# An xLSTM block, a top-2 expert layer and an ELU feed-forward on one core: summed logits in PSUM, a repeated block of 64 columns, more work allowed on GpSimd, and a new order

## The chip, the cores and the metric

The kernel runs on one core of one Trainium2 chip. The metric is the device time of one execution in microseconds (us); less is better. The time before is the median of three runs.

## The reference, cut to what matters

Three layers follow each other on 1536 tokens of 320 values: a gated linear attention (2 batches, 8 heads, 768 steps, 40 wide), a router that sends each token to two of eight experts (320 x 1024 x 320), and a dense layer (320 x 2048 x 320) with an ELU.

```python
def _attn_ref(q, k, v, i_gate, f_gate, o_gate):
    for t in range(S):
        m_new = np.maximum(f_gate[:, :, t] + m, i_gate[:, :, t])
        f_stab = np.exp(f_gate[:, :, t] + m - m_new)
        i_stab = np.exp(i_gate[:, :, t] - m_new)
        C = f_stab * C + i_stab * np.einsum('bhd,bhe->bhde', vt, kt)
        n = f_stab * n + i_stab * kt
        y[:, :, t] = o * (C @ qt) / np.maximum(np.abs(n @ qt), 1.0)

def _moe_ref(x, w_gate, w_noise, noise, w1, w2):
    noisy_logits = x @ w_gate + np.log1p(np.exp(x @ w_noise)) * noise
    top2 = np.argpartition(-noisy_logits, 2, axis=1)[:, :2]
    ...
    out[mask] += top2_w[mask, k, None] * (np.maximum(x[mask] @ w1[e], 0) @ w2[e])

def _moe2_ref(x, w_in, w_out):
    h = x @ w_in
    return np.where(h > 0, h, np.exp(np.minimum(h, 0)) - 1) @ w_out
```

## The kernel before

Everything is computed with pairs of f16 numbers: a value is scaled by a power of two, rounded to f16 (the upper half, `high`, L386) and the rest is rounded again (the lower half, `low`, L395). A product is then two or three f16 matmuls into one sum.

**Attention.** The tokens are cut into 12 tiles of 128 (`attention(t)`, L659; tiles 0 to 5 are batch 0). Of each tile k and q are split (`k3`, `q3`), transposed on PE (L715, L716), copied out of PSUM (`kq`, L380 on ACT or L379 on DVE), multiplied (L718), masked (`pw`, L720 on DVE, or L721 on ACT and then L723 on GpSimd) and applied to `vw`, which is v times the exponential of the gates (L676, one DVE instruction `(va * SK*SV) * ewT`). A state `st` with its halves `s` and `slo` goes from tile to tile.

**Rows and logits.** `token_rows(t)` (L636) takes the finished rows `y`, finds the largest value of each row (`top`), makes a scale `sc` of it, and `split_row` (L594) writes `xr`, 640 columns of f16: 320 of upper halves, then the lower halves of the last 64 values, then those of the first 256. So five blocks of 128 columns come about, the middle one with 64 upper and 64 lower halves. The lower half needs two instructions, of 64 and of 256 columns. `xr` is written to `x_rows` in DRAM, from where the experts gather rows, and is transposed on PE (`turn_row`, L600); the copy `xTt` feeds five matmuls of 32 columns (L654) into a small piece of the PSUM bank `bank`, and DVE adds the two halves of these columns to 16 logits (L657). The transposes and `x_rows` use the same five blocks as the expert weights do (`BLK`, `PASSES`).

**Router.** After six tiles `router(hf)` (L785) scales the logits of that half (L803), takes softplus and noise, finds the two best experts, and makes tables of rows. It is a long chain of short DVE instructions with a few ACT ones and matmuls.

**Experts.** Weights come by DMA into four staging tiles `sw`, ACT or DVE rounds the upper half (L389, L390) and DVE makes the lower one (L400), giving `wa` and `wb`. `JOBS` lists 16 jobs (expert, half). A job gathers its rows (GpSimd, L991), multiplies by `wa` (L955), takes relu and its lower half (`hidden`, L1010 and L1012), multiplies by `wb` (L968 to L971).

**Last layer.** `mixed(b)` (L1121) gathers the two results of a token, adds them and splits the sum with the same `split_row` into `x3r`; then two products with `fwa` and `fwb`. Their weights are doubles and are unpacked on the way (L1089 to L1095).

**Order.** Nothing is scheduled by the framework. Every step is recorded with the engines that may do it and an estimated cost (`ON` names the engines by letter: A is ACT, V is DVE, G is GpSimd). A planner makes an order and picks the engine of each step; its result is kept in the table `ORDER`, which the program follows. Each engine then takes its instructions strictly in that order. The eight steps `FILL` (L510) are matmuls whose result nobody reads; they stand between others early on.

Of the kernel before, what the change touches and what calls it, by code (L numbers as in the profile page):

```python
# [14 lines left out]
I32 = mybir.dt.int32  # L15
# [25 lines left out]
BLK = ((0, P), (P, P), (2 * P, DM - 2 * P))  # L41
# [11 lines left out]
ON = dict(k3="A", q3="AV", vw="V", s3h="AV", s3l="V", ph="A", pl="GV", vh="VA", vl="V", y="VG", xr="AVG", turn="AV",  # L53
          kq="AV", yo="VA", wh="AV", hv="VA", wl="V", q3l="V")
# [19 lines left out]
c-jTQZ3KdOf&lR6{q_I6zdz6ad7g%rmWGaomX?-2G_*9dw6v?GqoJdrp`oLpqoJjxrKLL^9W5;_9St3QXii5<OG`^jLq|g&I=a))hx`2ygg|0Q1c@V6q=i  # L74
lp21y__B!wiAG15ThNC&N<D|C$lB#mT{EV4kR$Og?JTeObk5gS<|8>E2bu_n?+TF58Z740HL<b{^7HB!Vz$PO)Id$fXlhnA2#+CgsE8$F;~<bXWTCt5|@*
Z?`ASL{oyhaeb%m5~8f!5Hj>?vW=pLmt@QP=Ngw>)?Ilj(v+Bkqc7AWUPkOu`c!%Ho|mV$82njO|TgLKy;*zzOV-N#^QJzckmwC#}YWirdSW}<DX+)9O7S
KE98t^kvZN#5j=?#cm%VF8J5BsJVJbcNAWo}z&H31U*HR@kNyDr2EQXCe2K@fCz8e$e1})i1u@2TLco{U3SZ+0y2Abgn-g&?O2mjAGQlB{!L!63j}spgCE
|o+@hSdB)<h0J;72?`#K}CKBz}(rbb$VX7$RkKNvw!Gu^|#z5<B53VuPLW3PGSpqCi~mPw*;n#fRuO#EyuOX-r0cOw@?~#M<ajh#T@(;!niS@Sk7_GD)t<
4VfZ$SdqBlbz+Y-h%-?nA)=!tJcVVkCUGHJ#0b6P2ck{9kYD0eyhA+jE3qTDWR3he`48lcD3kw0jL|#sE3$(3hz5Bl|A%}KIqXR^$uxPy4p;<b(Er2#ioJ
+B-Xg1HhI|uI^o`f>K2f4R!x6HJ?#UNUkPHdY5i=l?Xq!A^1aZOQ=#XgQEqqL{1Rww@lQ#LUM3s^WNKT0v5h0^wmVA;3l|Y;5n3<qCvPhMwpOO=1%4E<A^  # L80
`;IaN!_Uj^*wncPvnf5GYe+Pte7>kVYW<%Jd-=-N$r^~HKM+v{+Y5-86mg}$xsIdP)DXl)hUF2lP9K2o|!(?pnBvdWDLD91M0!Ns5Cl7o78`kJzAy^;>on
A8Om^7x=&817o$^C>O1l`BthHMn_=iI3h4x$M-g^F6D*`Yp!@WYDxiS=h%TZL>bE3hMuf~UY?PW&b81MZ=p{X(0sAE-(>6OIW0cG;D4pHWIvJ&ZOpoapy`
=t;`kG$T8TwE3hg5`_&?_oV{|gD(EFEDJ)S8Mi2RhDds3bL|b<Uw<Op2P4Gdf2nm~W`R(2z@^6EaO@8H4_aNilhPPM+u-x}gj7j@r^O?qep+6zMDT2l|h6
hMJ>)B=bxOosoI&6J}4HX~31}BlQcq$lRDalVL9OlC02Ix=JUxEVV#O%!>S&%2PM`K;7vY{h;f#&6Sx7vqTHj|I#V0%Dm_rbEdwfPSl%j(qGUSuEZ6%54k
H<XFg*H24MixWLnIPDspXFVX|z8mU)J0GaW`}8g!2-a}n;>Oq#Qq0TboA%#g{kzv8mokjt}CHo@h%0$XHDY?-aFRkp^~*#_HWTddCSxINe8+U$WFaUC|sw
# [226 lines left out]
def tile_mlstm_moe_ffn(  # L312
# [105 lines left out]
    def a_(shape, dt, name, n=2):  # L418
        return buf(lambda: attn_pool[-1], shape, dt, name, n)
# [89 lines left out]
    for _ in range(FILL):  # L509
        te(3, 384, lambda: [PE.matmul(bank[:, :384], ones16(), ones16()[:, None].to_broadcast([P, 3, P]),  # L510
                                      start=True, stop=True) for _ in range(3)])
    vec(1, lambda: V.memset(mt()[:, 0:1], -1e30), [], [mt[0]])

    def gates(g):
# [25 lines left out]
        act(n, lambda: A.activation(ewT()[:, ts], ewT()[:, ts], AF.Exp), [ewT[g]], [ewT[g]], "exp")  # L540
        act(n, lambda: A.activation(mnT()[:, ts], rows(p2()), AF.Exp), [p2], [mnT[g]], "exp")
# [891 lines left out]
```

## Time and profile before

| | us |
|---|---|
| median of 3 runs | 456.63 (455.63 to 457.31) |
| the profiled execution | 455.6 |
| its span, first to last instruction | 453.9 |
| PE busy in the span | 435.4 (96%) |
| PE weight loads | 369.6 (81%) |
| DVE busy | 380.4 (84%) |
| ACT busy | 300.1 (66%) |
| GpSimd (POOL) busy | 87.7 (19%) |

Busy time is the time in which an engine has at least one instruction in work. The duration of one instruction holds its start and its end, which overlap with its neighbours; the step from one start to the next is shorter. The granted clock is the share of full speed (1.00 is 2.4 GHz, 0.50 is 1.2 GHz) that TensorE had in a stretch.

### The profile page before, as it was taken

How to read it: one execution, taken by the hardware profiler on the slowest of the kernel's cores; microseconds unless marked ns; L12 is line 12 of the kernel's file. 1: busy time of each engine (PE TensorE's matmuls, PEld its weight loads, DVE VectorE, ACT ScalarE, POOL GpSimd, SP SyncE). 2: the span in 40 equal slices, each digit the busy share in tenths (PEclk: the TensorE clock that was granted, in tenths of full speed). 3: DMA queues.
4: the chain of work that ended last, by engine and by line, in shares of the span. 5: the costliest groups of instructions: out<-in, count | busy, mean ns of one | idle time of the engine just before them, and what ended most of it. 6: DMA issues, size and time to landing. Idle time of an engine off the chain costs nothing.

```text
span 453.9 us, 10600 instructions
## 1 busy us (share of the span) xinstructions
PE 435.4 (96%) x4098; PEld 369.6 (81%) x4098; DVE 380.4 (84%) x874; ACT 300.1 (66%) x523; POOL 87.7 (19%) x103
## 2 busy tenths in 40 slices
PE   8999898789899999999999999999999999999994
PEld 6889688677788898889888889878878788878873
DVE  6899999989899889997989887798777678769861
ACT  4999998866767555665644445688677785746630
POOL 3133015205111130201212005305121400000000
PEclk9999999699999999999999999999999999999998
DMA  9798888778986999889999643323213111010001
GB/s 147 122 158 164 163 198 214 208 201 264 258 244 182 231 266 267 199 267 233 253 250 240 194 134 108 99 32 80 81 45 45 48 40 32 1 43 30 16 16 37
DMA packets 99120, 65.89 MB, mean 145 GB/s; under 512 B 75008, under 2 KB 90678, under 8 KB 99062
## 3 DMA queue, kind: packets, MB, share of 16 engines
q1 hardware_dynamic: 96182, 56.75, 51.7%
q0 software_dynamic: 2848, 8.34, 6.6%
q8 instruction: 34, 0.56, 0.5%
q14 instruction: 24, 0.20, 0.1%
q10 hardware_dynamic: 32, 0.05, 0.0%
HBM read 50.87 MB, written 8.52 MB: 131 GB/s over the span
## 4 chain that ended last, share of the span: by engine, by line
PE 67%; DVE 8%; DMA 4%; ACT 3%; issue 1%; SPq 0%; DVEq 0%; ACTq 0%
PE S L955 33%; PE O L968 12%; PE O L969 12%; PE O L971 11%; DMA sw<-in_moe_w 3%; DVE wa L400 1%; DMA sf<-in_moe_w_in 1%; DVE hidden L1012 1%; DVE wb L400 1%; ACT nm L1090 1%; DVE fwa L400 1%; DVE nm L384 1%; ACT wa L389 1%; ACT nm L1089 1%; DVE na L1091 1%
## 5 line engine op out<-in xcount | busy, mean ns | idle before, releaser
L955 PE MATMUL S<-xT,wa 128*128 128x224 f16 (+1 forms) x1024 | 99.9, 256 | 2.7 <-DVE hidden L1012 1.4
L955 PEld LDWEIGHTS <-wa 128*128 128x128 f16 x1024 | 93.7, 99 | 6.6 <-DVE hidden L1012 2.4
L955 PE MATMUL S<-x3T,fwa 128*128 128x256 f16 x768 | 88.2, 273 | 0.0
L955 PEld LDWEIGHTS <-fwa 128*128 128x128 f16 x768 | 75.2, 98 | 10.1
L968 PE MATMUL O<-wb,hidden 128*128 128x320 f16 (+1 forms) x256 | 75.4, 299 | 0.0
L969 PE MATMUL O<-wb,hidden 128*128 128x320 f16 (+1 forms) x256 | 75.3, 299 | 0.0
L991 POOL DMA_INDIRECT xg<-x_rows,table x32 | 36.9, 1152 | 120.4 <-DMA xT<-xg 89.7
L971 PE MATMUL O<-wb,hidden 128*128 128x320 f16 (+1 forms) x200 | 59.8, 299 | 0.0
L968 PE MATMUL O<-fwb,gh 128*128 128x320 f16 x192 | 57.4, 299 | 0.0
L969 PE MATMUL O<-fwb,gh 128*128 128x320 f16 x192 | 57.4, 299 | 0.0
L1010 ACT ACTIVATE hidden<-S 128x448 f16<-128x448 f32 (+1 forms) x64 | 31.9, 510 | 21.3 <-PE S L955 20.5
L1012 DVE SCALAR_TENSOR_TENSOR hidden<-S,hidden 128x128 f16<-128x128 f32 (+2 forms) x92 | 40.1, 455 | 5.2 <-ACT hidden L1010 5.0
L1173 DVE SCALAR_TENSOR_TENSOR ex<-ex,th 128x512 f32<-128x512 f32 x48 | 33.0, 687 | 13.2 <-ACT ex L1171 11.1
L1170 ACT ACTIVATE th<-S,sca 128x512 f32<-128x512 f32 x48 | 32.8, 691 | 16.0 <-PE S L955 16.0
L1172 ACT ACTIVATE re<-S,sca 128x512 f32<-128x512 f32 x48 | 32.8, 687 | 15.8 <-PE S L955 5.3
L1171 ACT ACTIVATE ex<-S,sca 128x512 f32<-128x512 f32 x48 | 33.0, 689 | 9.6 <-PE S L955 5.1
L1174 DVE SCALAR_TENSOR_TENSOR re<-ex,re 128x512 f32<-128x512 f32 x48 | 33.1, 692 | 3.2 <-ACT re L1172 1.2
L969 PEld LDWEIGHTS <-hidden 128*128 128x128 f16 (+1 forms) x256 | 26.9, 105 | 6.9
L968 PEld LDWEIGHTS <-hidden 128*128 128x128 f16 (+1 forms) x256 | 26.8, 105 | 6.9
L400 DVE SCALAR_TENSOR_TENSOR wa<-sw,wa 128x1024 f16<-128x1024 f32 x24 | 29.0, 1219 | 2.3 <-ACT wa L389 2.2
L1133 POOL DMA_INDIRECT yg<-y_rows,rows_i x24 | 25.1, 1044 | 28.8 <-ACT x L1138 8.8
L753 PE MATMUL O<-vw,pw 128*128 128x56 f32 (+2 forms) x192 | 29.2, 294 | 0.2 <-DVE pw L720 0.2
(248 smaller groups left out, 842.2 us busy)
## 6 DMA issues: line engine op xcount, KB each, us to landing
sw<-in_moe_w SPq DMA_DIRECT2D x16, 512.0 KB, 5.1
sw<-in_moe_w SPq DMA_DIRECT2D x16, 480.0 KB, 4.1
sf<-in_moe_w_out SPq DMA_DIRECT2D x16, 320.0 KB
sw<-in_moe_w SPq DMA_DIRECT2D x16, 256.0 KB, 5.3
sf<-in_moe_w_in SPq DMA_DIRECT2D x8, 512.0 KB
sw<-in_moe_w SPq DMA_DIRECT2D x8, 320.0 KB, 5.8
y_rows<-yo SPq DMA_DIRECT2D x16, 160.0 KB, 3.2
sf<-in_moe_w_in SPq DMA_DIRECT2D x8, 256.0 KB
```

Source lines behind the costliest of these rows:

```text
L400: some(on, [("V", 0.07 + 0.06 * m + 1.04e-3 * n, lambda: V.scalar_tensor_tensor(dst(), src(), scale(), hi(), op0=OP.mult, op1=OP.subtract) ...
L955: PE.matmul(acc, wa[:, r, w, f * P:(f + 1) * P], xT[:, j, :n], start=(i == 0), stop=(i == 7))
L968: PE.matmul(o, a, wb[:, 0, f % FB], start=(f == 0), stop=False)
L969: PE.matmul(o, a, wb[:, 1, f % FB], start=False, stop=(not b and f == last))
L971: PE.matmul(o, b[0], wb[:, 0, f % FB], start=False, stop=(f == last))
L991: do([("G", 1.1, lambda: G.indirect_dma_start(out=xg()[:n], out_offset=None, in_=(x_all if hf else x_rows[0]())[:, :], in_offset=bass.Indi ...
L1012: vec(2 * n, lambda x=x, n0=n0, n=n: V.scalar_tensor_tensor(hi(x, n), src(n0, n), 0.0, hi(n0, n), op0=OP.max, op1=OP.subtract), [ph, hid[f ...
L1170: act(512, lambda: A.activation(th(), pf(), AF.Tanh, scale=sca()[:, 2:3]), [pf, sca], [th], "exp", 1)
L1171: act(512, lambda: A.activation(ex(), pf(), AF.Exp, scale=sca()[:, 1:2]), [pf, sca], [ex], "exp", 1)
L1172: act(512, lambda: A.activation(re(), pf(), AF.Relu, scale=sca()[:, 1:2]), [pf, sca], [re], m=1)
L1173: vec(512, lambda: V.scalar_tensor_tensor(ex(), ex(), 1.0, th(), op0=OP.add, op1=OP.mult), [ex, th], [ex], port=True)
L1174: vec(512, lambda: V.scalar_tensor_tensor(re(), ex(), 0.0, re(), op0=OP.min, op1=OP.add), [ex, re], [re], port=True)
```

## The change

1. **Logits in PSUM.** Each tile has 16 columns of `bank` of its own (`sums`), into which eight matmuls of 16 columns add up (`PASSES`, as for the experts; the product of lower half and lower half is left out). The reduction on DVE goes; the scaling of the half reads PSUM. The `FILL` matmuls have 192 columns instead of 384 and twice their number, since the bank's first 192 columns are taken.
2. **A second copy of 64 columns.** The blocks begin at column 64 now, and the odd block is the first 64 values. `xr` has 704 columns: 320 upper halves, a copy of the first 64 of them (`dup`, on GpSimd or ACT), and 320 lower halves by one instruction. Columns 64 to 703 are stored and transposed: 640 as before.
3. **`vw` without its constant.** The gates `ewT` are scaled once per half by DVE, so that `vw` is a plain product, which GpSimd may do too. GpSimd may also round `q3` and the weights' upper halves; the planner's cost for rounding on GpSimd is raised.
4. **Order.** A new `ORDER`.

```diff
-BLK = ((0, P), (P, P), (2 * P, DM - 2 * P))
+TM = DM - 2 * P
+BLK = ((TM, P), (TM + P, P), (0, TM))
...
-ON = dict(k3="A", q3="AV", vw="V", ...
-          kq="AV", yo="VA", wh="AV", hv="VA", wl="V", q3l="V")
+ON = dict(k3="A", q3="AVG", vw="VG", ...
+          kq="AV", yo="VA", wh="AVG", hv="VA", wl="V", q3l="V", dup="GA")
...
 ORDER = """
-c-jTQZ3KdOf&lR6{q_I6zdz6ad7g%rmWGaomX?-2G_*9dw6v?GqoJdrp`oLpqoJjx
+c-jrq{RjGaf&lQ(^XL6}etLhNA8KjnXlZC^Y3WNxLrX(LLqkJHLqkJHM?*(LM?*t
...
-                  ("G", 0.14 + 0.09 * m + 0.87e-3 * n,
+                  ("G", 0.13 + 2.0e-3 * n,
...
-        te(3, 384, lambda: [PE.matmul(bank[:, :384], ones16(), ones16()[:, None].to_broadcast([P, 3, P]),
-                                      start=True, stop=True) for _ in range(3)])
+        te(6, 192, lambda: [PE.matmul(bank[:, 192:384], ones16(), ones16()[:, None, :64].to_broadcast([P, 3, 64]),
+                                      start=True, stop=True) for _ in range(6)])
...
         act(n, lambda: A.activation(ewT()[:, ts], ewT()[:, ts], AF.Exp), [ewT[g]], [ewT[g]], "exp")
+        vec(n, lambda: V.tensor_scalar(ewT()[:, ts], ewT()[:, ts], SK * SV, None, op0=OP.mult), [ewT[g]], [ewT[g]])
...
-        for i, (o, c, n) in enumerate(((DM, 2 * P, tm), (DM + tm, 0, 2 * P))):
-            low(n, lambda o=o, n=n: xr()[:, o:o + n], lambda c=c, n=n: x()[:, c:c + n], scale,
-                lambda c=c, n=n: xr()[:, c:c + n], [*r, xr[0]], [xr[i + 1]], on="V" if scale else "VG", m=bool(scale))
+        some(ON["dup"], [("G", 0.25, lambda: G.tensor_copy(xr()[:, DM:DM + TM], xr()[:, :TM])),
+                         ("A", 0.17, lambda: A.activation(xr()[:, DM:DM + TM], xr()[:, :TM], AF.Copy)),
+                         ("V", 0.12, lambda: V.tensor_copy(xr()[:, DM:DM + TM], xr()[:, :TM]), True)], [xr[0]], [xr[1]])
+        low(DM, lambda: xr()[:, DM + TM:], x, scale, lambda: xr()[:, :DM], [*r, xr[0]], [xr[2]],
+            on="V" if scale else "VG", m=bool(scale))
...
-        load(lambda: [(x_rows[b]()[c * P:(c + 1) * P], xr())], [x_rows[b]], [xr])
-        xT, lg = a_([P, 5, P], F16, "xTt"), ps_l()
-        turn_row(xr, P, xT, 0, [xr], [xT], True)
-        def logit():
-            for j, r in enumerate((0, 1, 2, 0, 1)):
-                PE.matmul(lg()[:, :4 * E], xT()[:, j], rwt()[:, r].rearrange("p w e -> p (w e)"), start=(j == 0), stop=(j == 4))
-        te(5, 4 * E, logit, [xT, rwt], [lg])
-        vec(4 * E, lambda: V.tensor_reduce(logits()[:, t], lg()[:, :4 * E].rearrange("p (w e) -> p e w", w=2),
-                                           axis=AX.X, op=OP.add), [lg], [logits[b]])
+        load(lambda: [(x_rows[b]()[c * P:(c + 1) * P], xr()[:, TM:])], [x_rows[b]], [xr])
+        xT = a_([P, 5, P], F16, "xTt")
+        turn_row(xr, P, xT, 0, [xr], [xT], True, TM)
+        te(len(PASSES), 2 * E, lambda: [
+            PE.matmul(sums()[:, t], xT()[:, j], rwt()[:, r, w], start=(i == 0), stop=(i == len(PASSES) - 1))
+            for i, (j, w, r) in enumerate(PASSES)], [xT, rwt], [sums[t]])
...
-        vec(n1, lambda: V.scalar_tensor_tensor(vw(), va(), SK * SV, ewT()[:, row(t)].unsqueeze(2).to_broadcast([P, H, D1]),
-                                               op0=OP.mult, op1=OP.mult), [va, ewT[half_of(t)]], [vw_], port=True)
+        mul(n1, vw, va, lambda: ewT()[:, row(t)].unsqueeze(2).to_broadcast([P, H, D1]), [va, ewT[half_of(t)]], [vw_], on=ON["vw"])
```

Two places of the new order follow; names are tiles, with the number of the buffer. The first is GpSimd's queue in the first third of the attention. Before:

```order
L701 DMA s_620<-s_620 40x328
L370 DMA rw<-in_moe_w_gate 128x2x8
L384 TENSOR_TENSOR yb_92<-y_594,sg 128x320
L392 TENSOR_SCALAR xr<-yb_91,sc 128x320
L723 AFFINE_SELECT pw<-pw 128x512
L392 TENSOR_SCALAR xr<-yb_92,sc 128x320
L392 TENSOR_SCALAR xr<-yb_90,sc 128x320
```

GpSimd's queue of the changed kernel in the same third:

```order
L392 TENSOR_SCALAR q_287<-qt 128x8x80
L370 DMA rw<-in_moe_w_gate 64x8
L384 TENSOR_TENSOR vw_97<-va_94,ewT 128x328
L720 AFFINE_SELECT pw<-pw 128x512
L384 TENSOR_TENSOR vw_98<-va_95,ewT 128x328
L370 DMA rw<-in_moe_w_noise 64x8 x2
```

Seven of the twelve `vw` and one `q3` stand on GpSimd now; the four roundings of `xr` and one forwarding DMA of `s` have left it.

The second place is DVE's queue at the end of the attention, up to the scaling of the second half's logits, on which the second router waits. Before:

```order
L645 TENSOR_SCALAR sc<-top 128x1
L657 TENSOR_REDUCE logits<-bank 128x16
L379 COPY xT<-T 128x5x128
L801 TENSOR_SCALAR inv_140<-top 128x6
L657 TENSOR_REDUCE logits<-bank 128x16
L400 SCALAR_TENSOR_TENSOR xr<-yb_92,sc,xr 128x64
L400 SCALAR_TENSOR_TENSOR xr<-yb_92,sc,xr 128x256
L400 SCALAR_TENSOR_TENSOR wb<-sw,wb 128x960
L657 TENSOR_REDUCE logits<-bank 128x16
L400 SCALAR_TENSOR_TENSOR wa<-sw,wa 128x1024
L657 TENSOR_REDUCE logits<-bank 128x16
L803 SCALAR_TENSOR_TENSOR logits<-logits,inv_140 128x96
```

DVE's queue of the changed kernel, up to the same scaling:

```order
L645 TENSOR_REDUCE top<-yb_92 128x1
L648 TENSOR_SCALAR sc<-top 128x1
L798 TENSOR_SCALAR inv_140<-top 128x6
L379 COPY xTt<-T 128x640
L400 SCALAR_TENSOR_TENSOR xr<-yb_91,sc,xr 128x320
L400 SCALAR_TENSOR_TENSOR xr<-yb_92,sc,xr 128x320
L862 TENSOR_TENSOR rh_164<-starts,as_166 128x192
L379 COPY xTt<-T 128x640
L400 SCALAR_TENSOR_TENSOR wa<-sw,wa 128x1024
L800 SCALAR_TENSOR_TENSOR logits<-bank,inv_140 128x96
```

The reductions are gone and the two pieces of each lower half are one; two copies `xTt`, which ACT made before, stand here.

## Rows read from the trace of the kernel before

**Rows 1.** Stretches of the span: us, then busy time of PE, PEld, DVE, ACT, POOL; PEclk; DMA share; GB/s.

```profile
10.00:30.00 20.00, 19.96 (x271) 17.69 (x270) 17.58 (x48) 17.75 (x34) 3.62 (x6) 1.00 0.86 143
30.00:60.00 30.00, 27.23 (x371) 24.13 (x371) 28.20 (x101) 29.22 (x50) 7.32 (x10) 1.00 0.86 161
60.00:79.00 19.00, 17.39 (x223) 16.35 (x221) 18.93 (x68) 16.95 (x33) 7.17 (x8) 1.00 0.83 213
79.00:85.00 6.00, 3.24 (x45) 2.27 (x43) 5.89 (x19) 5.62 (x12) 1.68 (x2) 0.78 0.59 173
85.00:100.00 15.00, 13.71 (x136) 11.76 (x136) 13.28 (x43) 10.11 (x15) 1.09 (x1) 0.86 0.83 215
100.00:122.00 22.00, 19.82 (x204) 16.10 (x202) 19.86 (x47) 14.36 (x23) 6.79 (x6) 1.00 0.94 244
...
145.00:440.00 295.00, 295.00 (x2564) 250.26 (x2562) 244.24 (x468) 185.95 (x326) 52.97 (x54) 1.00 0.49 127
```

**Rows 2.** Waits of PE, 11 to 86 us: who waited for whom, total us, times, longest.

```profile
PE bank L654 <- ACT xTt L380: 1.5, 3, 0.8
PE S L718 <- ACT kq L380: 1.2, 2, 0.7
PE T L607 <- ACT xTt L380: 1.1, 2, 0.6
...
PE bank L654 <- DVE logits L657: 0.7, 3, 0.3
```

**Rows 3.** Groups of DVE, shapes apart: count, busy us, mean ns of one, idle before.

```profile
L720 DVE TENSOR_TENSOR pw<-S,causal 128x512 f32<-128x512 f32 x16 | 10.6, 665 | 0.1
...
L400 DVE SCALAR_TENSOR_TENSOR xr<-yb,sc,xr 128x256 f16<-128x256 f32 x12 | 6.1, 506 | 0.0
...
L676 DVE SCALAR_TENSOR_TENSOR vw<-va,ewT 128x328 f32<-128x328 f32 x12 | 5.8, 487 | 0.0
L400 DVE SCALAR_TENSOR_TENSOR k<-kt,k 128x320 f16<-128x320 f32 x12 | 5.8, 480 | 0.0
...
L400 DVE SCALAR_TENSOR_TENSOR xr<-yb,sc,xr 128x64 f16<-128x64 f32 x12 | 3.8, 321 | 0.0
...
L657 DVE TENSOR_REDUCE logits<-bank 128x16 f32<-128x32 f32 x12 | 2.2, 185 | 0.4 <-PE bank L654 0.4
...
L390 DVE TENSOR_SCALAR x3r<-x 128x320 f16<-128x320 f32 x6 | 2.0, 330 | 0.1
...
L379 DVE COPY xTt<-T 128x640 f16<-128x640 f16 x1 | 0.5, 492 | 0.0
```

**Rows 4.** Groups of ACT, shapes apart.

```profile
L389 ACT ACTIVATE q<-qt 128x640 f16<-128x640 f32 x11 | 8.0, 731 | 0.0
...
L380 ACT ACTIVATE xTt<-T 128x640 f16<-128x640 f16 x11 | 7.6, 696 | 0.2
...
L721 ACT ACTIVATE pw<-S 128x512 f32<-128x512 f32 x8 | 4.8, 597 | 0.1
...
L389 ACT ACTIVATE s<-st 40x328 f16<-40x328 f32 x10 | 4.6, 464 | 0.9 <-DVE st L694 0.9
L389 ACT ACTIVATE xr<-yb,sc 128x320 f16<-128x320 f32 x8 | 4.5, 558 | 0.9 <-DVE sc L645 0.7 <-issue 0.2
```

**Rows 5.** PE in order of time near 78 us: start, us from first start to last end, count.

```profile
78.37 0.28 PE L654 MATMUL bank<-rwt,xTt 128*128 128x32 f16 x5
78.49 0.72 PE L607 MATMUL T<-id,xr 128*128 128x128 f16 x10
```

**Rows 6.** Groups of POOL, shapes apart.

```profile
L384 POOL TENSOR_TENSOR yb<-y,sg 128x320 f32<-128x320 f32 x2 | 1.8, 914 | 8.0 <-issue 4.7 <-ACT sg L634 3.3
```

**Rows 7.** DVE and POOL in order of time near 73 us: start, us.

```profile
72.74 1.20 DVE L400 SCALAR_TENSOR_TENSOR wa<-sw,wa 128x1024 f16<-128x1024 f32 x1
...
73.26 1.18 POOL L723 TENSOR_SCALAR_AFFINE_SELECT pw<-pw 128x512 f32<-128x512 f32 x1 [1.24 <-ACT pw L721]
73.87 0.91 DVE L384 TENSOR_TENSOR yb<-y,sg 128x320 f32<-128x320 f32 x1
```

More of the change, by code (lines that the diff above doesn't have):

```diff
@@ L111 @@
+U9b-x{xf*`FW(CBK{0d)kkBg#haQ0!iiYH%9!iFYP$U!!#Y2e@3`!vo;zLTP5rUy|C>6?t(xGf97kW2T2sJ~MP&L#FwL`T~Co~NG1E5D$`~
 """
@@ L556, in tile_mlstm_moe_ffn @@
     spill = fixed([P, E, 2], F32, "spill")
-    tm = DM - 2 * P
     def router_setup():
         for c0, w in ((0, w_gate), (E, w_noise)):
-            load(lambda c0=c0, w=w: [(rw()[:, 0:2, c0:c0 + E], w[:2 * P].rearrange("(j p) e -> p j e", p=P))],
+            load(lambda c0=c0, w=w: [(rw()[:, 0:2, c0:c0 + E], w[TM:].rearrange("(j p) e -> p j e", p=P))],
                  [rw], dma=0.14, q="G")
-            for d0 in range(0, P, tm):
-                load(lambda c0=c0, w=w, d0=d0: [(rw()[d0:d0 + tm, 2, c0:c0 + E], w[2 * P:])], [rw], dma=0.04, q="G")
+            for d0 in range(0, P, TM):
+                load(lambda c0=c0, w=w, d0=d0: [(rw()[d0:d0 + TM, 2, c0:c0 + E], w[:TM])], [rw], dma=0.04, q="G")
         due, do.due = do.due, DUE["nz"]
@@ L606, in turn_row @@
         pt = ps_t()
-        te(5, P, lambda: [PE.transpose(pt()[:, x, :n], xr()[:n, x * P:(x + 1) * P], id16()[:n, :n])
+        te(5, P, lambda: [PE.transpose(pt()[:, x, :n], xr()[:n, o + x * P:o + (x + 1) * P], id16()[:n, :n])
                           for x in range(5)], r, [pt], [x[0] if isinstance(x, tuple) else x for x in w])
@@ L802, in router @@
                                         op0=OP.bitwise_and), [top[t] for t in range(hf * HT, hf * HT + HT)], [inv2[hf]])
-        vec(100, lambda: V.scalar_tensor_tensor(logits()[:, ts], logits()[:, ts], 0.5 / SW, bc(inv2()[:, ts], 2 * E),
-                                                op0=OP.mult, op1=OP.mult), [logits[hf], inv2[hf]], [logits[hf]], port=True)
+        vec(100, lambda: V.scalar_tensor_tensor(logits()[:, ts], sums()[:, ts], 0.5 / SW, bc(inv2()[:, ts], 2 * E),
+                                                op0=OP.mult, op1=OP.mult),
+            [*(sums[t] for t in range(hf * HT, hf * HT + HT)), inv2[hf]], [logits[hf]], port=True)
         act(50, lambda: A.activation(nl, logits()[:, ts, E:], AF.Sigmoid, scale=-1.0), [logits[hf]], [me], "sigmoid")
@@ L1136, in tile_ @@
                    [rows_i[hf], y_rows[hf], opened], [yg[j]], late=1.7, dma=0.75)
-            x3, xr = l_([P, DM], F32, "x3"), l_([P, ROW], F16, "x3r")
+            x3, xr = l_([P, DM], F32, "x3"), l_([P, ROW + TM], F16, "x3r")
             act(DM, lambda: A.activation(x3(), yg[0](), AF.Copy, scale=cw()[:, t, 0:1]), [yg[0], cw[hf]], [x3], m=1)
@@ L1141, in tile_ @@
             split_row(xr, x3, None, [x3])
-            turn_row(xr, P, xT, n0, [xr], [xT[n0]], not b)
+            turn_row(xr, P, xT, n0, [xr], [xT[n0]], not b, TM)
         for i in range(2):
@@ L1213, in tile_mlstm_moe_ffn @@
     do.cls = 1
-    do([("PE", 0.0, open_late)], [logits, *x_rows], [opened])
+    do([("PE", 0.0, open_late)], [sums, *x_rows], [opened])
     do.due = DUE["sc"]
@@ L1329, in full_attention @@
                 pc, vw = ps_o(), a_([P, H, D1], F32, "vw", 1)
-                vec(n1, lambda: V.scalar_tensor_tensor(vw(), va(), SK * SV, wide(ewT()[:, row(t)]),
-                                                               op0=OP.mult, op1=OP.mult), [va, ewT], [vw])
+                vec(n1, lambda: V.tensor_tensor(vw(), va(), wide(ewT()[:, row(t)]), op=OP.mult), [va, ewT], [vw])
                 te(H, 4 * D1, lambda: [PE.matmul(heads_of(pc()[:D])[:, h], kt()[:, h], vw()[:, h], start=True, stop=True)
@@ L1374, in summed @@
         def summed(t):
[L1375 removed]
+            ci, xr = a_([P, 1], F32, "ci"), a_([P, ROW + TM], F16, "xr", 4)
             vec(1, lambda: V.tensor_mul(ci(), inv2()[:, t:t + 1], sca()[:, 0:1]), [inv2, sca], [ci])
             split_row(xr, lambda: acc()[:, t], ci, [acc, ci])
[L1378 removed]
+            load(lambda: [(x_rows[t // HT]()[t % HT * P:(t % HT + 1) * P], xr()[:, TM:])], [x_rows[t // HT]], [xr])
         def taken(b):
```

83 lines of the change are left out of this document (40 added, 43 removed).

## The prediction

> **What bounds the kernel now.** I read the stretches of the span first, then PE's waits, then the groups of DVE, ACT and GpSimd by shape, and last two short pieces in order of time. The stretches [rows 1] show two kernels in one. From 145 to 440 us PE is busy for 295.00 of 295 us at full clock: whatever ends there is bound by PE's own work, which this change leaves as it is. Before that PE has holes: 2.8 us in 30 to 60, 1.6 in 60 to 79, 2.8 in 79 to 85, 1.3 in 85 to 100 and 2.2 in 100 to 122. A microsecond saved before 145 is kept to the end if it closes a hole, and only then. In 10 to 30 there is no hole to close (19.96 of 20).
>
> Who makes the holes of the attention is in two views. In 30 to 60 ACT is busy for 29.22 of 30 us and DVE for 28.20; in 60 to 79 DVE for 18.93 of 19 [rows 1]. Both are nearly full, and each waits for the other. PE's longest waits up to 86 us are for ACT (1.5, 1.2 and 1.1 us); the first for DVE is 0.7, by the logits for the small piece of PSUM that the reduction has to clear [rows 2]. So the change must be counted on both engines, on equal work.
>
> The granted clock is 0.78 in 79 to 85 and 0.86 in 85 to 100 [rows 1]. At two levels, 1.2 and 2.4 GHz, that is 0.22 x 6 x 2 + 0.14 x 15 x 2 = 6.8 us at the lower one; it begins in the stretch with PE's widest holes.
>
> **The change part by part.** Durations overlap their neighbours: `wa` lasts 1.20 us, but the next instruction starts 1.13 after it [rows 7], so I take 0.07 off each to get a step.
>
> DVE, attention only. Seven `vw` leave for GpSimd: 7 x (0.487 - 0.07) = 2.9 us [rows 3]. Twelve reductions go: 12 x (0.185 - 0.07) = 1.4. The lower halves: 12 x (0.506 + 0.321 - 0.14) = 8.2 become 12 of 320 columns, which I price by the lower half of `k`, the same operation on as many columns, 12 x (0.480 - 0.07) = 4.9; saved 3.3. Together 7.6. The new order puts on DVE: three roundings of `xr` and three of `s`, priced by the rounding of `x3r`, 6 x 0.26 = 1.6; two `pw`, 2 x 0.60 = 1.2; two `xTt`, 2 x 0.42 = 0.8; one `q3`, one `top`, one `yb`, priced by `xTt`, 1.3; two scalings of `ewT`, priced by the reduction, 0.2. Together 5.1. **Net: DVE is 2.5 us lighter.**
>
> ACT, attention only. Two `q3` (1.3), two `xTt` (1.3), two `pw` (1.1), three `s` (1.2) and one `top` (0.4, as `s`) leave: 5.3 us [rows 4]. One `xr` (0.5) comes, and eight of the twelve copies of 64 columns. No row shows such a copy. From 320 to 640 columns the rows grow from 0.558 to 0.731, so 0.00054 us a column; from the 0.464 of `s` down to 64 columns that is 0.33, a step of 0.25. The bounds are 0 (it falls into a wait) and the 0.39 of `s` itself; I take 0.25, 2.0 in all. **Net: ACT is 2.8 us lighter.**
>
> GpSimd gets 7 x 0.91 us [rows 6] and gives up its four `xr`; it was busy for 7.3 of 30 and 7.2 of 19 us [rows 1], so its own time costs nothing. If that cover fails it is by being late for `vw`, on which PE's next product waits. The forwarding of `s` that leaves it joins the nine on SP, at nothing.
>
> PE. Five matmuls of 32 columns are followed by the next group after 0.12 us [rows 5], 24 ns each; that is too short for the columns to matter, so I price 16 columns the same. Eight instead of five cost 0.07 a tile, 0.9 us for twelve. The bounds are 0.9, all on the path, and 0, where they stand behind a wait; six of the twelve tiles come after the last heads, where PE has 2.8 us of holes, so I take half, 0.45. The `FILL` columns are the same in number.
>
> Where the time goes on the path: the relief counts outside 10 to 30 alone, 55 of the 75 us between 10 and 85, that is 0.73 of it. The mean of 2.5 and 2.8 times 0.73 is 1.95. The wait of 0.7 for the PSUM piece goes with the piece. The sum: -1.95 - 0.7 + 0.45 = **-2.2 us**. Its bounds: a relief of 0.9 (the new order gives half back) to 2.8 (all of ACT's), the 0.7, and PE's 0.9 to 0 make -0.7 to -3.5.
>
> After 85 us the order moves six roundings of weights from DVE to ACT, which is busy for 10.11 of 15 and 14.36 of 22 us there [rows 1]; at nothing. In the last layer the lower half in one instruction and its copy are covered by PE's 295.00 of 295.
>
> The profiled execution took 455.6 us, 1.0 under the median of the runs, 456.63. I take the difference to the median: 456.6 - 2.2 = 454.4. A measurement of this kernel can tell about 0.5%, 2.3 us, from no change.
>
> The shared port speaks against the change. A mask on GpSimd began at 73.26 and ended at 74.44; the `yb` of DVE, which began at 73.87, took 0.91 us and ended 0.34 after it, where a product of as many columns takes 0.48 [rows 3, 7]. So a DVE instruction lost 0.43 to one on GpSimd. The sum above lets the seven `vw` fall where DVE reads PSUM; the third rival is what happens otherwise. The Trainium skill, page SBUF — State Buffer, section Who interferes with whom, says that a DVE instruction with two SBUF inputs contends with a GpSimd instruction that reads SBUF, and that the one that comes second blocks until the first is done. By that rule the sum would be the third rival's; the trace's row agrees with it for the mask, and no run here shows it for `vw`.
>
> **The rivals.**
>
> *The clock stays up.* If PE idles less before 85, the 6.8 us at the lower clock may not come. PE's work in them would take half the time: 3.4 us less at most, 451.0. For it: the dip follows the largest holes. Against it: the six tiles after the last heads still go through transpose, copy and product one after the other.
>
> *The relief is lost behind the weights.* The DMA share rises to 0.83 and 0.94 in 85 to 122 while PE still has 3.5 us of holes [rows 1]. If the weights' loads pace that stretch, a router that ends 2 us earlier only makes those holes longer, and PE's added 0.45 stays: about 457.0. Against it: the share is 0.59 in 79 to 85, so a load can start sooner if its staging tile is free sooner.
>
> *GpSimd holds the port.* This one ends slower. Seven `vw` and the `q3` on GpSimd, each with 0.91 us in which DVE may not start an instruction with two inputs: at 0.43 each, as in the row, DVE loses 3.4 us, and at 0.91 each 7.3. Its net of -2.5 turns to +0.9 or +4.8. The first leaves ACT's relief without use, no change; the second is 4.8 x 0.73 - 0.7 + 0.45 = +3.3, 459.9. It decides from 0.31 us a piece, where DVE's gain is gone; for 2.3 us slower, 0.75 are needed. For it: in 60 to 79 DVE has 0.07 us left. Against it: DVE's `pw`, `y`, `st` and `den` read PSUM, and the planner holds the port for the length of each GpSimd step.
>
> **How the numbers follow.** My forecast, -2.2 with its bounds (453.1 to 455.9), has 0.48: 0.30 of it beyond 2.3 us faster, as the middle lies almost on that edge and the longer half below it is filled by a tighter order, 0.16 within, and 0.02 for an order that is worse in itself. The clock rival has 0.13, all faster. The weights have 0.19: 0.17 within, 0.02 slower. The port has 0.20: 0.17 slower, 0.03 within. Faster 0.43, within 0.36, slower 0.21. The forecast's own range is 453.1 to 455.9; the range of 8 in 10 reaches down to the clock rival's and up into the port rival's: 450.8 to 459.0.
>
> **What would show it.** Right: in 30 to 85 PE's holes shrink from 7.2 to about 5 us; no wait for `logits`; the lower halves at some 0.48 us; the first expert matmul about 2 us earlier; 24 ns a step for the products of 16 columns. Wrong: DVE instructions of 0.9 us beside `vw` on GpSimd, PE waiting for `vw`; a granted clock under 1.00 in other stretches than 79 to 100; holes in 85 to 122 that grow by what the attention saved; any hole of PE after 145.

## The result, and the profile after

The changed kernel takes **458.19 us** (median of 13 runs, 456.39 to 463.07) where the kernel before takes 455.63 (13 runs beside them, 454.65 to 457.31). The ratio is 1.0072, with a 95% interval of 1.0051 to 1.0093: **slower by 0.7%**. The medians are 2.6 us apart and the means 3.3, where the prediction had 2.2 us faster. The profiled execution took 457.31 us with a span of 455.6, near the fast end of its runs; three of the 13 took 461 to 463. In this document the ratios leave out runs in the chip's slower state, the medians do not.

The stretches of the span of the changed kernel (columns as in [rows 1]):

```profile
10.00:30.00 20.00, 20.00 (x264) 17.96 (x263) 17.59 (x46) 17.13 (x31) 5.86 (x9) 1.00 0.80 134
30.00:60.00 30.00, 28.00 (x400) 25.34 (x398) 28.33 (x93) 28.15 (x50) 7.98 (x11) 1.00 0.90 169
60.00:79.00 19.00, 18.33 (x241) 17.24 (x240) 18.72 (x67) 17.66 (x37) 8.44 (x9) 1.00 0.77 191
79.00:85.00 6.00, 4.27 (x60) 3.63 (x61) 5.82 (x14) 5.71 (x12) 2.82 (x3) 0.68 0.64 198
85.00:100.00 15.00, 13.40 (x142) 11.43 (x141) 13.92 (x44) 10.25 (x16) 0.00 (x0) 0.90 0.83 246
100.00:122.00 22.00, 19.45 (x204) 16.21 (x202) 19.06 (x47) 15.28 (x25) 6.69 (x6) 1.00 0.98 278
...
145.00:440.00 295.00, 294.21 (x2556) 249.13 (x2554) 241.78 (x458) 189.54 (x337) 50.99 (x49) 1.00 0.48 124
```

Against [rows 1], PE's holes shrink by 0.77 us in 30 to 60, by 0.94 in 60 to 79 and by 1.03 in 79 to 85, **2.74 us together**. They grow by 0.31 in 85 to 100 and by 0.37 in 100 to 122, where the DMA share rises from 0.94 to 0.98, and from 145 us on, where there was none, there are 0.79.

The waits of PE in the changed kernel, from 11 to 86 us, from 85 to 122 and from 145 to 440, the longest of each:

```profile
PE S L715 <- ACT kq L380: 1.1, 2, 0.9
PE T L610 <- ACT xT L380: 1.0, 1, 1.0
PE bank L655 <- DVE xTt L379: 0.6, 2, 0.4
...
PE S L953 <- ACT hidden L1008: 1.9, 1, 1.9
PE S L953 <- DVE hidden L1010: 1.4, 3, 0.7
...
PE O L966 <- ACT yo L380: 0.8, 1, 0.8
```

Of [rows 2] the wait for `logits` is gone and the waits for `xTt` are small. From 85 to 122 us PE waited for DVE's `hidden` in the kernel before as well:

```profile
PE S L955 <- DVE hidden L1012: 1.4, 3, 0.9
```

New are the 1.9 us for ACT's `hidden` there, and the 0.8 us for `yo` from 145 us on, where PE waited for nothing before.

The largest loss is behind the last product. DVE at the end of the changed kernel, then DVE of the kernel before, in order of time (start, us):

```profile
447.73 0.55 DVE L1187 TENSOR_SCALAR zo<-O,sca 128x320 f32<-128x320 f32 x1 [1.08 <-PE O L969]
448.20 0.15 DVE L1240 TENSOR_TENSOR flag<-most,least 128x1 int32<-128x1 f32 x1
```
```profile
440.98 0.15 DVE L1242 TENSOR_TENSOR flag<-most,least 128x1 int32<-128x1 f32 x1
...
448.11 0.55 DVE L1189 TENSOR_SCALAR zo<-O,sca 128x320 f32<-128x320 f32 x1 [1.08 <-PE O L971]
```

`flag` says whether the exact path must run, and every engine loads it and branches on it. Before, it is written 7 us ahead of the last `zo`; the new order makes it DVE's last instruction. The records of loads and branches, which the views leave out, show PE's branch from 446.08 to 449.56 before and from 448.98 to 452.85 after. From the end of the last `zo` to the end of the span it is 5.24 us before and 7.33 after, **2.1 us more**. PE's last product ends at 448.07 before and at 447.69 after: up to there the change is 0.4 us ahead. So 0.4 won and 2.1 lost is the 1.7 us by which the two profiled executions differ (455.6 and 457.31 us). The medians of the runs are 2.6 us apart; the other 0.9 us stands in no profile.

The prices, from the groups of DVE, ACT and POOL with shapes apart (count, busy us, mean ns):

```profile
L400 DVE SCALAR_TENSOR_TENSOR xr<-yb,sc,xr 128x320 f16<-128x320 f32 x12 | 6.1, 530 | 0.0
```
```profile
L598 ACT ACTIVATE xr<-xr x8: 240/246/257, 35.8 to 81.4; 128x64 f16<-128x64 f16 x8
L597 POOL COPY xr<-xr x4: 237/334/1246, 31.7 to 76.1; 128x64 f16<-128x64 f16 x4
```
```profile
L384 POOL TENSOR_TENSOR vw<-va,ewT 128x328 f32<-128x328 f32 x7 | 5.6, 800 | 11.0 <-DVE ewT L541 4.4 <-PE O L753 4.3 <-DMA va<-in_v 2.3
```

(The second fence is the view of the tile `xr`: shortest, median and longest ns.) The lower half was priced at 0.48 us and takes 0.53, the copy on ACT at 0.33 and takes 0.25, `vw` on GpSimd at 0.91 and takes 0.80.

### The profile page after: what moved, and what is told of

Read it like the earlier page. It is cut to its first block, busy times and chain, and to the rows that moved or that the text cites. A ratio compares the mean times of both kernels' runs of the same rounds, so it can differ in the third digit from the quotient of the medians.

```text
span 455.6 us, 10726 instructions
## 1 busy us (share of the span) xinstructions
PE 435.6 (96%) x4158; PEld 372.8 (82%) x4158; DVE 376.9 (83%) x846; ACT 303.3 (67%) x537; POOL 91.6 (20%) x103
## 4 chain that ended last, share of the span: by engine, by line
PE 64%; DVE 10%; DMA 5%; ACT 3%; issue 2%; SPq 0%; DVEq 0%; ACTq 0%
PE S L953 31%; PE O L966 11%; PE O L967 11%; PE O L969 10%; DMA sw<-in_moe_w 3%; DMA sf<-in_moe_w_in 2%; DVE hidden L1010 1%; DVE wa L400 1%; DVE fwa L400 1%; DVE nm L384 1%; DVE na L1091 1%; DVE wb L400 1%; DVE na L1089 1%; ACT nm L1088 1%; ACT nm L1087 1%
## 5 line engine op out<-in xcount | busy, mean ns | idle before, releaser
L989 POOL DMA_INDIRECT xg<-x_rows,table x32 | 38.8, 1212 | 105.5 <-DMA xT<-xg 72.4
L1087 ACT ACTIVATE nm<-sf 128x320 f32<-128x320 f32 (+1 forms) x28 | 16.2, 578 | 23.9 <-DVE fwb L400 12.1
```

What stands on the lines that cost most here:

```text
L989: do([("G", 1.1, lambda: G.indirect_dma_start(out=xg()[:n], out_offset=None, in_=(x_all if hf else x_rows[0]())[:, :], in_offset=bass.Indi ...
```

## The experiments

All kernels of one group ran on one chip, each beside the kernel before. Five groups of runs fell on five chips, here B to F. The chip of the result above is not on record; it is called A here. No chip has two groups, so what is said of a chip below could also belong to its group of runs. The kernel before has medians of 455.05 and 455.56 us on B and C, and of 457.74, 457.88 and 458.30 on D, E and F.

**The flag and the port (chip B).** In the changed kernel the step that writes `flag` goes behind the step of the judge ahead of it (written at 356.95 us); in the kernel before it goes to the very end; on top of the first, one `FILL` step is moved to the start, or all twelve `vw` go to DVE.

```
flag_early, flag_fill, flag_vw:   + flag (behind the judge's step before it)   - flag (last of ORDER)
before_flag_late:                 - flag (441 us)                              + flag (last of ORDER)
flag_fill also:  FILL step 4 to behind FILL step 1        flag_vw also:  seven vw: way G -> way V
```

> The changed kernel with one step of its order moved: the last step of the judge, which writes the flag that all engines read before the final branch, stands right after the step before it (about two thirds through the order) and not as the very last instruction of DVE. Theory 'tail': the changed kernel's last matmul ends at 447.7 us, 0.4 earlier than before's 448.1, and its span is longer only because the flag is written at 448.2, so that PE's branch runs from 449.0 to 452.9 after everything else; with the flag early the end is bound by the last output again, the span falls from 455.6 to about 453.5 and the time to 0.4 us under to 0.7 us over the kernel before. Rival 'body': the new order loses in the body of the kernel, in executions unlike the profiled one; then the time stays 2 us or more over the kernel before and only the branch moves.

> The kernel before with the step that writes the flag moved to the very end of its order, as it stands in the changed kernel; nothing else. Theory 'tail': DVE writes the flag at about 448.8, PE's branch of 3.5 to 3.9 us starts at about 449.5 and ends at about 453.2, and the time is 1.7 to 2.6 us over the kernel before. Rival 'body': no change beyond 0.5 us.

> As flag_early, and one of the fill steps that stands later in the order follows the first fill step at the start, so that PE gets 12 and not 6 matmuls of 192 columns there, as many columns as before. Theory 'start': the changed kernel's clock rises at 12.9 us and not at 10.7 because fewer columns stand at the start, which costs PE 1.5 us in the first 30 us; here the clock rises at about 10.7 and the span is 0.5 to 1.5 us under that of flag_early. Rival: the start is bound by loads and gates; the clock rises earlier and the time stays within 0.4 us of flag_early.

> As flag_early, and all twelve vw stand on DVE, at their places of the order; seven of them were on GpSimd. Theory 'relief' (the prediction's): DVE gets 7 x 0.42 = 2.9 us more in the attention, of which some 2 reach the end: 1 to 2 us slower than flag_early. Rival 'port': GpSimd's vw held back DVE's instructions with two inputs by as much as they relieved it: within 0.5 us of flag_early, or faster.

Measured: flag_early 458.43 us, 1.0068 (1.0043 to 1.0093); before_flag_late 457.38, **1.0048** (1.0029 to 1.0067); flag_fill 457.60, 1.0055 (1.0038 to 1.0073); flag_vw 457.59, 1.0052 (1.0036 to 1.0069). The late flag alone costs the kernel before 0.5%, 2.2 us, with a tail of 7.40 us from the last `zo` to the end: the tail is real, as theory 'tail' has it. With the flag early the tail of the changed kernel is 5.46 us, and yet the time does not fall: it stays 3 us over the kernel before, as rival 'body' has it. In that profile PE's holes from 145 us on are 2.5 us, and its last product ends at 448.67 us, 1.0 later than in the changed kernel's. flag_fill misses its theory: PE's holes up to 30 us fall from 2.7 to 1.9, but the clock rises at 12.79 us and the time is that of flag_early within the intervals. `vw` on DVE or on GpSimd is the same within the intervals, so the seven `vw` on GpSimd are not the loss.

**The parts without the order (chip C).** The logits in PSUM, the copy with the one lower half, and both, each in the order of the kernel before: the reductions are struck out of it, the copy takes the place of the lower half of 64 columns and the rest that of the one of 256.

```diff
 before_logits, before_parts:
-        te(5, 4 * E, logit, [xT, rwt], [lg])
-        vec(4 * E, lambda: V.tensor_reduce(logits()[:, t], ...
+        te(len(PASSES), 2 * E, lambda: [PE.matmul(sums()[:, t], ...
 before_lower, before_parts:
-        for i, (o, c, n) in enumerate(((DM, 2 * P, tm), (DM + tm, 0, 2 * P))): low(n, ...
+        some(ON["dup"], ...), low(DM, ...
```

> The kernel before in its own order, with one part of the change: the router's logits add up in PSUM (eight products of 16 columns, the twelve reductions go). Theory 'order' (the parts help, the new order gives it back): DVE 1.4 us lighter in the attention, worth about 1.0, and the logits wait of 0.7 gone, against 0.45 to 0.9 of PE's: 0.8 to 1.2 us faster than before, and the holes of PE in 30 to 85 us smaller. Theory 'weights' (the loads of the experts' weights pace PE from 85 us on, whatever the attention saves): the first expert matmul earlier by up to 1 us, the holes in 85 to 122 larger by the same, the time within 0.5 us of before. Theory 'parts' (the added products cost more than they save): slower by 0.5 to 1 us.

> The kernel before in its own order, with the other part alone: a copy of 64 columns in each row (on ACT or GpSimd as in the changed kernel) and the lower half in one instruction. DVE 3.3 us lighter in the attention, ACT 2.0 heavier. Theory 'order': 0.5 to 1.5 us faster. Theory 'weights': first expert matmul earlier, holes in 85 to 122 larger by as much, time within 0.5 us of before. Theory 'parts': ACT, the fuller engine in 30 to 60, sets the pace there: PE's holes in 30 to 60 grow by about 1 us and the kernel is 0.5 to 1.5 us slower.

> Both parts in the order of the kernel before, with the vw products, the roundings and the flag where they stood: the change without its new order. Theory 'order': 1.5 to 2.5 us faster than before, which would make it the fastest of all. Theory 'weights': within 0.7 us of before, the holes of PE in 85 to 122 larger by what 30 to 85 saved. Theory 'parts': slower by 1 to 2.5 us.

Measured: before_logits 455.35 us, 0.9989 (0.9970 to 1.0009); before_lower 456.73, 1.0025 (1.0007 to 1.0043); before_parts 456.05, 1.0011 (0.9989 to 1.0032). **None of the three is faster by more than can be told**, and before_lower is slower by 0.25%, 1.1 us, with its interval just clear of 1. That is what theory 'parts' gave for it, but not for its reason: PE's holes in 30 to 60 are 2.73 us, as before (2.77). The other two times are as theory 'weights' had them, but its sign did not come either: in before_logits the first expert matmul starts at 85.14 us, 0.2 later than before. The stretches of before_parts show what the parts do to the engines:

```profile
30.00:60.00 30.00, 27.70 (x400) 25.17 (x399) 27.04 (x89) 29.84 (x54) 8.24 (x11) 1.00 0.87 165
60.00:79.00 19.00, 17.60 (x230) 16.56 (x228) 18.54 (x64) 17.40 (x36) 6.37 (x9) 1.00 0.86 211
```

Against [rows 1] DVE is lighter by 1.16 and 0.39 us, but ACT, which has the copies, heavier by 0.62 and 0.45. PE gains 0.68 us of busy time in the two (0.37 of it in before_logits already), and its holes in 30 to 85 are 6.66 us against 7.14. So the rest of the 2.74 us that the changed kernel wins there should come from its order, with the `vw` on GpSimd. That is a subtraction; no run has the new order without the parts.

**The steps behind a wait (chip C).** In flag_early ACT and PE near 157 us are:

```profile
156.24 0.69 ACT L1085 ACTIVATE nm<-sf 128x512 f32<-128x512 f32 x1 [1.72 <-DMA sf<-in_moe_w_in]
156.96 0.73 ACT L1086 ACTIVATE nm<-nm,edge 128x512 f32<-128x512 f32 x1
157.59 0.95 ACT L1006 ACTIVATE hidden<-S 128x448 f16<-128x448 f32 x2
158.44 0.43 ACT L378 ACTIVATE yo<-O 128x320 f32<-128x320 f32 x1
```
```profile
158.93 0.30 PE L964 MATMUL O<-wb,hidden 128*128 128x320 f16 x1 [1.08 <-ACT yo L378]
```

ACT stands for 1.72 us at the first step of a fused-layer weight whose load has not landed, and that weight is wanted at 286 us. Two `hidden` and a `yo` stand behind it, and PE behind them. In the kernel before ACT meets such a load late as well, and for longer, but `yo` stands ahead of it and PE has no hole:

```profile
156.84 0.44 ACT L380 ACTIVATE yo<-O 128x320 f32<-128x320 f32 x1 [0.54 <-PE O L971]
160.20 0.68 ACT L1089 ACTIVATE nm<-sf 128x512 f32<-128x512 f32 x1 [2.93 <-DMA sf<-in_moe_w_in]
```

The next experiment moves these five steps (with the two `hidden` of DVE) ahead:

```diff
+ACT hidden, ACT hidden, DVE hidden, DVE hidden, ACT yo
 DVE na<-sf, ACT nm<-sf, ... (the fused-layer weight)
-ACT hidden, ACT hidden, DVE hidden, DVE hidden, ACT yo
```

> The changed kernel with the flag early, and at 156 us five steps (two hidden on ACT, two on DVE, one yo on ACT) moved ahead of the rounding of a fused-layer weight, which waits there for its DMA. Theory 'order': the holes of PE from 145 to 440 us fall from 2.5 us to under 1 and the kernel is 1 to 2 us faster than the one with the flag early alone (456.5 to 457.5 where that had 458.4). Rival 'weights': the experts' weights themselves are late there, the holes only move by a few us, 458.4 within 0.7.

Measured: **455.05 us, 0.9985** (0.9965 to 1.0006), 0.8% better than flag_early, but on another chip, on which neither flag_early nor the changed kernel ran. The same place of ACT in its trace:

```profile
155.82 0.55 ACT L1006 ACTIVATE hidden<-S 128x448 f16<-128x448 f32 x1 [1.78 <-PE S L951]
156.26 0.43 ACT L378 ACTIVATE yo<-O 128x320 f32<-128x320 f32 x1
156.58 0.67 ACT L1085 ACTIVATE nm<-sf 128x512 f32<-128x512 f32 x1
```

`yo` comes 2.2 us earlier and PE has no hole there. One of 1.3 us is left, at 186 us, of the same kind. A kernel that also moves that step ahead ran on chip E (461.85 us, 1.0080), but it computes wrong values, so its time is no evidence.

**Both moves crossed (chips D and E), and what the chips do.** The four kernels with and without each move ran together on D; the changed kernel, the one with both moves, and the kernel before again on E.

> The changed kernel as it is, beside the three others on one chip, so that the place of the flag and the place of the five steps at 156 us are crossed. If the two costs are separate: this one is the slowest, 1.006 to 1.008 of before.

> The changed kernel with the five steps at 156 us moved ahead of the wait for the DMA, and the flag still last. If the two costs are separate: 2.0 to 2.5 us slower than the one with both mended, 1.002 to 1.005 of before, and a tail of about 7.3 us after the last product's end, as in the changed kernel. If only the tail counts: as the changed kernel, 1.007. If only the five steps count: as with both mended, 0.998.

> The flag early and the five steps as in the changed kernel. If the two costs are separate: 2.0 us faster than the changed kernel, 1.002 to 1.004 of before. If the first measurement of it (1.0068) holds: the early flag saves the tail and gives it back before 200 us; holes of PE after 145 of 2 us and more.

> Both mended. If the two costs are separate: the fastest of the four, 0.997 to 1.000 of before; the difference to the one with the flag early alone is what the five steps cost, 1 to 3 us.

> The kernel before once more, for its profile on the same chip as the next three. If the stops of PE with nothing to wait for at the start of the fused layer (285 to 290 us in the last four runs, 0.7 us an instruction, then the lower clock) belong to that chip and not to the order, a chip without them shows none here and none in the three others; a chip with them shows them here too.

> The changed kernel as it is, on one chip with the mended ones: 1.005 to 1.009 of before if no such stops come, 1.010 to 1.015 if they come.

> The changed kernel with the flag early and the five steps at 156 us ahead of the wait. If the tail (2.1 us) and the holes from 145 us on are the loss: 2 to 4 us faster than the changed kernel beside it, 0.997 to 1.001 of before. If the loss is the new order as a whole: within 1.5 us of the changed kernel.

| kernel | chip D | chip E |
|---|---|---|
| before again | | 457.78, 0.9979 (0.9951 to 1.0008) |
| changed | 464.68, 1.0120 (1.0074 to 1.0167) | 466.01, 1.0175 (1.0142 to 1.0209) |
| five steps moved | 464.34, 1.0140 (1.0101 to 1.0180) | |
| flag early | 463.74, 1.0106 (1.0073 to 1.0139) | |
| both | 461.77, 1.0084 (1.0049 to 1.0119) | 461.66, 1.0073 (1.0048 to 1.0099) |

The two moves together win **4.4 us on E**, by medians whose intervals lie apart. On D the ratios give 1.6 us, and their intervals overlap. One move alone is not told from none on D; with the other in place the flag brings 2.6 us there and the steps 2.0, by the medians. The profiles do show two separate costs: the tail is 5.4 us with the flag early and 7.3 without, and PE's holes from 145 to 280 us are 1.7 us with the steps behind the wait (flag early) and 0.0 to 0.2 with them ahead.

That the steps moved alone win nothing has a reason on record, the granted clock of the runs. Its mean is 0.980 for them and 0.985 to 0.986 for the other three. An estimate: at a mean clock c a span T holds 2 x (1 - c) x T at the lower level, of which half is lost at most; so about 2.5 us of that kernel's time can be the clock. Why its clock was lower stays open. Both kernels without the late flag were expected at 1.004 or less, and both are slower than that: the two costs are not the whole loss.

The kernel before against itself gives 0.9979, so 0.2% is what chance does here. But the changed kernel loses more on D and E than on A, and both moves do not bring it back. The profiles show a third cost, at the start of the last layer, called fused in the expectations. PE in after_yo on chip D, in order of time:

```profile
283.06 0.62 PE L608 MATMUL T<-id,x3r 128*128 128x128 f16 x5
283.86 0.22 PE L608 MATMUL T<-id,x3r 128*128 128x128 f16 x1 [0.19 <-issue]
285.28 0.27 PE L608 MATMUL T<-id,x3r 128*128 128x128 f16 x2 [1.21 <-issue]
286.01 0.22 PE L608 MATMUL T<-id,x3r 128*128 128x128 f16 x1 [0.46 <-issue]
286.70 0.23 PE L608 MATMUL T<-id,x3r 128*128 128x128 f16 x1 [0.48 <-issue]
```

The rows that it transposes are ready at 283.7; PE waits for nothing that the trace shows, and does one step in 0.7 us. In all profiles of the changed order on D and E such stops make 2.7 to 3.3 us of holes from 280 to 300, and on D the granted clock then falls to its lower level for 3.4 us, from 288 us at the earliest. On B and C the changed order has at most 0.11 us there, in the profile on A 0.02. The stretch from 280 to 300 us of the kernel before, of the changed one and of the one with both moves, all on chip E, and of the last on chip C:

```profile
280.00:300.00 20.00, 18.72 (x162) 15.52 (x160) 12.78 (x33) 10.60 (x19) 8.64 (x10) 1.00 0.33 94
```
```profile
280.00:300.00 20.00, 16.80 (x139) 13.25 (x138) 9.71 (x25) 8.90 (x19) 8.75 (x10) 1.00 0.27 75
```
```profile
280.00:300.00 20.00, 16.68 (x139) 13.35 (x138) 10.79 (x23) 10.37 (x22) 8.77 (x9) 1.00 0.22 59
```
```profile
280.00:300.00 20.00, 19.98 (x173) 16.75 (x172) 14.52 (x32) 13.82 (x28) 10.08 (x10) 1.00 0.33 91
```

So the stops come on some chips only, and on E the changed order has 2 us more of them than the order before (3.2 us of holes against 1.3, one profile each). The runs' granted clock is lower there too: 0.982 for the changed kernel and 0.986 with both moves, where the kernel before beside them has 0.9895. By the estimate above that is 3.4 and 1.6 us at most. With the 2 us of stops it would make up the 3.9 us between both moves and the kernel before; the profiles do not show it, since that of the kernel before is of the slowest of its 8 runs (460.46 us).

**The start, and the logits again (chip F).** yo_fill is the kernel with both moves and a `FILL` step moved to the start as in flag_fill; before_logits_copy is before_logits on another chip.

> The changed kernel with the flag early, the five steps at 156 us ahead of the wait, and one of the FILL steps moved from later to the start. If the losses add up one by one, 0.8 us of PE's idle time before 30 us goes too: 0.996 to 0.999 of before on a chip where PE does not stop at the start of the fused layer, and faster than both kernels by 0.5 to 2 us; 1.004 to 1.008 on one where it does. If the start is hidden by the later waits: as with the two mends, 0.9985 or 1.0075.

> The logits' part alone in the order of the kernel before, a second time, to see whether its 0.9989 holds on another chip: 0.997 to 1.001 if the part is worth up to 1 us everywhere; above 1.003 if its 36 added products move PE's instructions so that PE stops longer at the start of the fused layer, on a chip where it does.

Measured: yo_fill 462.0 us, 1.0096 (1.0065 to 1.0128); before_logits_copy 457.13, 0.9981 (0.9954 to 1.0007). F has the stops too: 3.4 us of holes from 280 to 300 in yo_fill, 0.8 in before_logits_copy. The step at the start is not seen to win anything (both moves without it gave 1.0084 and 1.0073, on other chips), and the 36 added products alone do not lengthen the stops: they are long with the new order. **No version beats both kernels by more than can be told.** The nearest is the logits' part alone, 0.9989 and 0.9981, both intervals with 1 inside.

## Why the prediction was wrong, point by point

*The relief of the attention was right.* PE's holes in 30 to 85 were to shrink from 7.2 to about 5 us; they are 4.4. The wait for `logits` is gone, and the first expert matmul starts at 83.83 us, 1.1 earlier than before (84.97), where 2 were forecast. Some of what is missing went at the start: PE's holes up to 30 us grow from 1.9 to 2.7. The prediction had priced the start at nothing because the `FILL` columns are the same in number; their place is another, and flag_fill, which moves some back, has 1.9 us again, though its time is not better. The clock rises to its upper level at 12.89 us instead of 10.67, but that is not shown to be the change: it rises at 12.35 in the kernel before again (chip E), at 11.07 in flag_early and at 12.79 in flag_fill.

*The reason for the relief was half wrong.* The sum credited the removed reductions and the wider lower half; before_parts shows that these, with the copies that ACT has to make, are worth 0.5 us of holes and nothing in the time. The moves between engines in the order should have given the rest, by the subtraction above. PE's added products were rightly priced: eight of 16 columns, from 80.50 us, take 0.35 us where five of 32 took 0.28 [rows 5], 0.07 more a tile.

*The step that failed is "everything behind 85 us at nothing".* The prediction says that what ends after 145 us "is bound by PE's own work, which this change leaves as it is"; the change has a new order there too. **The flag**: the order was read at the attention and not at its end, where the flag had gone from 7 us ahead of the last `zo` to behind it. It costs 2.1 us in the profile and 2.2 in before_flag_late; this is the part that a run shows by itself. **The covers of the weights**: 295.00 of 295 after 145 us [rows 1] was taken for cover that can hide anything; but an in-order engine that meets a late load holds back the `hidden` and `yo` behind it. ACT stands at the loads for the experts about as long as it did, from 85 to 122 us before and after:

```profile
ACT wa L389 <- DMA sw<-in_moe_w: 6.6, 3, 3.5
```
```profile
ACT wa L389 <- DMA sw<-in_moe_w: 7.0, 5, 2.7
```

The loads also come as much earlier as they are asked for: the 14th goes out at 93.73 us instead of 95.61 and ends ACT's wait at 104.06 instead of 106.29. What is new is what stands behind such a wait. ACT and PE in the changed kernel:

```profile
106.12 1.06 ACT L389 ACTIVATE wa<-sw 128x1024 f16<-128x1024 f32 x1 [1.00 <-DMA sw<-in_moe_w]
107.08 1.01 ACT L380 ACTIVATE xT<-T 128x640 f16<-128x640 f16 x2
107.98 0.87 ACT L1008 ACTIVATE hidden<-S 128x384 f16<-128x384 f32 x2
```
```profile
108.92 0.49 PE L953 MATMUL S<-xT,wa 128*128 128x192 f16 x4 [1.85 <-ACT hidden L1008]
```

The same comes again with `yo`, for which PE waits 0.77 us at 159.25. **The stops at 285 us** on some chips, 2 us more than before on E: the profile of the kernel before has no hole there, so it could not show them. Their cause, that of the lower clock on D and E, and the 0.9 us that no profile shows on A stay open.

*The rivals.* The relief lost behind the weights is what happened in part: 0.7 of 2.74 us went to the holes in 85 to 122, as that rival has it, and 0.8 to those from 145 on, of which it does not speak. So half of the relief was lost. With the tail its 457.0 would be 459.1, near the 458.19 measured; that is luck in part. The clock rival did not come: the dip at 81.16 us lasts 6.8 us as before. It lasts 3.4 in the profiles of flag_early, flag_vw and before_parts, so its length goes with neither kernel. GpSimd does hold the port, but does not decide: near 31 us POOL and DVE in the changed kernel are

```profile
30.76 0.99 POOL L384 TENSOR_TENSOR yb<-y,sg 128x320 f32<-128x320 f32 x1 [4.63 <-DMA s<-s]
31.70 1.25 POOL L597 COPY xr<-xr 128x64 f16<-128x64 f16 x1
```
```profile
30.93 0.99 DVE L390 TENSOR_SCALAR s<-st 40x328 f16<-40x328 f32 x1
31.86 0.47 DVE L400 SCALAR_TENSOR_TENSOR q<-qt,q 128x320 f16<-128x320 f32 x1
```

The rounding `s` on DVE takes 0.99 us beside the `yb` of GpSimd, where the two others of the same shape take 0.32 and 0.31, and the copy on GpSimd 1.25 beside DVE's next two, where its shortest takes 0.24. The Trainium skill, page SBUF — State Buffer, section Who interferes with whom, has the engine that comes second block until the first is done, for a DVE instruction with one input such as this rounding in the two-port modes only; the rows agree, both ways, but do not show the mode. Beside the seven `vw` of GpSimd the sign of this rival came once in full:

```profile
10.20 0.90 POOL L384 TENSOR_TENSOR vw<-va,ewT 128x328 f32<-128x328 f32 x1 [4.42 <-DVE ewT L541]
```
```profile
10.42 1.03 DVE L384 TENSOR_TENSOR vw<-va,ewT 128x328 f32<-128x328 f32 x1
```

This `vw` of DVE takes 1.03 us instead of 0.48. With three smaller delays DVE lost some 1.2 us beside the seven, about 0.2 a piece (an estimate, each against the median of its group), where the rival was to decide from 0.31. And flag_vw, with all `vw` back on DVE, is neither faster nor slower than flag_early by more than the intervals allow, so the seven `vw` are worth about nothing either way.

*The chances.* Of the 0.21 for slower, 0.17 stood on the port, which did not come, 0.02 on the weights, which came in part, and 0.02 on an order worse in itself, which is nearest to what came; no case held a loss at the end of the program. That 458.19 lies within 450.8 to 459.0 is luck: the port rival had drawn the upper bound.

## What to carry to other kernels

When a kernel's order is made anew, read the whole of it, and its last ten steps first: a step that everything branches on must not be the last. A busy PE is no cover for an in-order engine: where a step that waits for a DMA is wanted late, everything wanted soon goes ahead of it. And run a small gain on several chips: the same two kernels stood 0.7% apart in one group of runs and 1.7% in another.

## What the runs showed of the hardware

- PE's branch on the flag lasts 3.3 to 3.9 us in all profiles, where those of ACT, DVE, GpSimd and SP last under 0.1. In the kernel before PE comes to it while its last products still run (446.08 us, before their end at 448.07); with the flag last it begins at 448.98 and all of it lies behind the end.
- On chips D, E and F PE does a step in 0.7 us for some steps at 284 to 293 us, waiting for nothing that the trace shows; in the profiles on A, B and C it does not. No run tells the cause. In the changed order the holes there are 2.7 to 3.4 us; on D and F the granted clock then fell to its lower level for 3.4 us, on E, with 3.2 and 3.3 us of holes, it did not.
- The same kernel does not always get the same clock. The kernel before has one stretch at the lower level within its work in its first profile (82.35 to 89.17 us) and two in its second (84.03 to 90.85 and 111.33 to 118.16).
